# Packed values times first-layer weights: one 64x32 matmul per head instead of one masked 128x64 matmul per pair of heads

## The chip, the core and the metric

The kernel runs on one core of a Trainium2 chip, in float32. The metric is the time of one execution in device microseconds. The engines are named as in the profile: PE (TensorE matmul) and PEld (its weight loads), DVE (VectorE), ACT (ScalarE), POOL (GpSimd) and SP (SyncE, which issues the DMAs).

## The reference

```python
def sm_attn(qq, kk, vv):                      # softmax attention, per batch and head
    s = scale * np.matmul(qq, kk.transpose(0, 1, 3, 2))
    a = np.exp(s - np.max(s, axis=-1, keepdims=True))
    a = a / (np.sum(a, axis=-1, keepdims=True) + 1e-09)
    return np.matmul(a, vv)
p_packed = sm_attn(p, k, v)                   # (8, 8, 32, 64): 8 batches, 8 heads, 32 packed rows
out = sm_attn(q, p_packed, p_packed)          # (8, 8, 576, 64)
x = out.transpose(0, 2, 1, 3).reshape(4608, 512)
h = x @ moe_w_in;   x = (h * np.cos(h)) @ moe_w_out              # 512 -> 2048 -> 512
h = x @ moe2_w_in;  y = (h * np.tanh(softplus(h))) @ moe2_w_out  # the same sizes
```

## The kernel before

**Stage one** covers the attention and the first feed-forward layer, **stage two** the second layer. The second attention has only 32 keys per head, so the kernel never forms `out`. It multiplies the packed values of every head with the head's 64 rows of `moe_w_in` first, which gives for each batch a matrix of 8 x 32 = 256 rows and 2048 columns, called W1 here. The hidden layer is then W1 transposed times the attention weights `aT` (256 x 288 for a half batch).

Stage one walks 256 steps: 16 half batches `t` of 288 tokens, 16 blocks `s` of 128 hidden columns each. A step issues the first product (`l1`, six 128x288 matmuls), the elementwise chain to h*cos(h), and the second product (`l2`, twelve matmuls) three steps later. All of them split float32 into a high and a low part and use three matmuls in `mm3` (lines 140 to 142). Background work is hung onto steps by tables of numbers (`at_pe`, `at_ew`, `at_ld`): the packed attention (`k_unit`, 16 units of one batch and four heads), the attention weights (`q_unit`), the conversion of weights, and the W1 products (`w_unit`). The order on each engine is not the order of the code: a scheduler that plays the program through a timeline places every instruction, with the priorities that `tc.high_priority` gives.

**The W1 products.** `k_unit` ends in stage `s6`: `xt` (128 x 128 in PSUM) holds the packed values of four heads transposed, its 64 value rows twice, one copy in partitions 0 to 63 and one in 64 to 127. Line 299 copies half of it to `PS` on ACT, for the scores of `q_unit` (line 354). Line 305 multiplies two 128x64 slices with `mask` on DVE into `PW`, in which a 128x64 block holds two heads block-diagonally. `w_unit` takes 128 rows of `moe_w_in` (two heads) and 512 columns, and multiplies a 128x64 block of `PW` with them (line 492). Two such matmuls, in the two 64-column halves of the array, fill one PSUM tile of the ring of four (`ring`, shared with `l1`, the scores and the transpositions): W1 of four heads (group `g`) and 512 columns (`fg`). Line 503 copies the tile to `wab` on ACT, line 504 takes the low part on DVE. In the table of groups by line one such matmul has two records.

For batch 0 the matmuls stand in the first steps, with freshly converted weights; for batch 1 around steps 28 to 40; batches 2 and 3, 4 and 5, 6 and 7 are made in pairs, with weights loaded back from DRAM (`ws`, `ld`), 8 sets a pair: a set is one `fg` and `g` for both batches, four matmuls, two PSUM tiles. In one set the two matmuls of a tile, and the first matmuls of the two tiles, use different halves of the array.

**Stage two** has 9 blocks of 512 tokens, 16 steps each: twelve 128x512 matmuls with moving operand `xr`/`xt` (blocks 0, 2, 4, 6, 8) or `xh` (blocks 1, 3, 5, 7), and twelve that accumulate with `wo` moving and `gh` stationary. `xh`, `gg` and `gh` lie in the pool `bpool`, opened when stage one's pool is closed, at the same place. In the built program `bpool` begins at byte 164352 of a partition (642 x 256) and `gap_b` takes its first 192 bytes, so that `gg`, `gh` and `xh` begin 192 bytes behind a multiple of 256; `xr`, `xt`, `wo` and `wab` begin at multiples of 256.

Of the kernel before, what the change touches and what calls it, by code (L numbers as in the profile page):

```python
# [8 lines left out]
F32 = mybir.dt.float32  # L9
F32R = mybir.dt.float32r  # L10
# [21 lines left out]
W_LD = 2  # L32
# [24 lines left out]
W_D = 0  # L57
# [18 lines left out]
PERM = ((0, 1, 2, 3), (2, 3, 0, 1))  # L76


def build(tc, q, k, v, p, w1i, w1o, w2i, w2o, out):
    nc = tc.nc  # L80
    ctx = ExitStack()
    with ctx:
# [29 lines left out]
        mask = wpool.tile([128, 64], F32, name="mask")  # L112
        nc.vector.memset(mask, 0.0)
        for a in range(2):
            nc.vector.memset(mask[64 * a : 64 * a + 64, 32 * a : 32 * a + 32], 1.0)
# [40 lines left out]
        PS = {}  # L156
        PW = {}
        lastexp = [None]

        def k_unit(b, g, alloc_v):  # L160
# [135 lines left out]
            def s6_ew():  # L296
                if b not in PS:
                    PS[b] = ap.tile([128, 128], F32, tag="psp", bufs=3, name=nm("psp"))
                nc.scalar.copy(PS[b][64 * g : 64 * g + 64], st["xt"][64 * g : 64 * g + 64, :128])
                if (b // 2, g) not in PW:  # L300
                    PW[(b // 2, g)] = ap.tile([128, 2, 2, D], F32, tag=f"pw{g}", bufs=2 - g, name=nm("pw"))
                pw = PW[(b // 2, g)]
                for sp in range(2):
                    i = sp if par == 0 else 1 - sp
                    nc.vector.tensor_tensor(pw[:, i, sp], st["xt"][:, 64 * sp : 64 * sp + 64], mask, ALU.mult)
# [14 lines left out]
        def q_unit(t, pre=None):  # L320
# [28 lines left out]
            def s2_pe():  # L349
                st["s"] = [ring() for _ in range(2)]  # L350
                for l in range(4):
                    h = PERM[b % 2][l]
                    for g in range(2):
                        nc.tensor.matmul(  # L354
                            st["s"][g][32 * l : 32 * l + 32, :TT],
                            PS[b][64 * g : 64 * g + 64, 32 * l : 32 * l + 32],
                            st["kt"][64 * g : 64 * g + 64, TT * h : TT * h + TT],
                            start=True,
                            stop=True,
                        )  # L360
# [103 lines left out]
        whalf = {}  # L464

        def w_unit(pair, fg, hp, bp, fresh=False, m=None):
            st = {} if m is None else m
            g, i = hp // 2, hp % 2
            cs = []

            if fresh:
                load, cs = conv(
                    w1i[128 * hp : 128 * hp + 128, 512 * fg : 512 * fg + 512],
                    [128, 512],
                    None,
                    lambda d: w1s.__setitem__((fg, hp), d),
                    "wo" if fg == 0 else True,
                    st,
                )
                cs = cs[:-1]  # L480
            else:

                def load():
                    st["m"] = ld_tile([128, 512])
                    nc.sync.dma_start(st["m"], w1s[(fg, hp)])

            def pe():
                if i == 0:
                    whalf[(bp, fg, g)] = ring()
                ps = whalf[(bp, fg, g)]  # L490
                pos = bp ^ i
                nc.tensor.matmul(  # L492
                    ps[64 * pos : 64 * pos + 64], PW[(pair, g)][:, i, pos], st["m"], start=True, stop=True
                )

            def ew():
                if i == 0:
                    return
                ps = whalf.pop((bp, fg, g))
                w = W1.get((2 * pair + bp, fg))  # L500
                if w is None:
                    w = W1[(2 * pair + bp, fg)] = wab_tile(bp, [128, 2, 2, 512], F32R)
                nc.scalar.copy(w[:, g, 0], ps)
                nc.vector.tensor_tensor(w[:, g, 1], ps, w[:, g, 0], ALU.subtract)

            return load, cs, pe, ew
# [99 lines left out]
        place(stages, [PRO + Q0_T + i for i in range(2)] + [PRO + Q0 + i for i in range(6)], HP_PRO)  # L606
        for j in range(16):
            load, cs, pe, ew = w_unit(0, j // 4, j % 4, 0, True)
            n = W0_STEP[j]
            at_ld(n - W0_LD if j >= 4 else PRO + W0E[j], load)  # L610
            for i, f in enumerate(cs):
                at_ew(n - 3 + i, f)
            at_pe(n, pe)
            at_ew(n, ew)
# [12 lines left out]
        for j in range(16):  # L627
            load, cs, pe, ew = w_unit(0, j // 4, j % 4, 1)
            n = W01[0] + int(W01[1] * j)
            at_ld(n - W_LD, load)  # L630
            at_pe(n, pe)
            at_ew(n, ew)
# [18 lines left out]
        for pair in range(3):  # L651
# [9 lines left out]
            for j in range(16):  # L661
                m = {}
                n = n0 + W_POS[pair][0] + int(W_POS[pair][1] * (j // 2 * 2 + 1))
                at_ld(n - W_LD - 1 + j % 2, w_unit(pair + 1, j // 4, j % 4, 0, m=m)[0])
                for bp in range(2):
                    _, _, pe, ew = w_unit(pair + 1, j // 4, j % 4, bp, m=m)
                    at_pe(n + W_D * bp, pe)
                    at_ew(n + W_D * bp, ew)
# [155 lines left out]
        bp.tile([128, 48], F32, name="gap_b")  # L824
# [90 lines left out]
```

## Time and profile before

| | us |
|---|---|
| median of 3 runs (1653.84 to 1654.74) | 1654.02 |
| the profiled execution | 1651.3 |
| its span, first to last instruction | 1649.5 |
| PE busy in it | 1588.2 |
| DVE, ACT, POOL busy | 717.9, 762.2, 365.0 |

The profiled execution is the one whose rows are read here; 1.8 us lie around its span. Stage one ends near 850 us of the span. PE is busy nearly without a break after the first 150 us; DVE and ACT are half busy in stage one and little in stage two. The DMA engines are nearly full for the first 150 us.

### The profile page before, as it was taken

What the parts mean: (1) busy time and instruction counts of PE and PEld (TensorE: products, weight loads), DVE (VectorE), ACT (ScalarE), POOL (GpSimd) and SP (SyncE); (2) the same over time, 40 slices, a digit from 0 to 9 for tenths busy, and PEclk for the clock granted to TensorE, in tenths of its full rate; (3) what the DMA queues carried; (4) which work ended last, traced back from release to release, by engine and by line L of the source; (5) the groups of instructions that cost most, each with busy time, mean ns of one, the idle gap of its engine ahead of it and who ended that gap; (6) DMA issues with size and microseconds to landing.
All of it is one profiled execution on the core that took longest, in us unless ns stands there. A gap on an engine that the chain in (4) does not pass through costs nothing.

```text
span 1649.5 us, 25389 instructions
## 1 busy us (share of the span) xinstructions
PE 1588.2 (96%) x9568; PEld 1324.5 (80%) x9568; DVE 717.9 (44%) x1529; ACT 762.2 (46%) x1510; POOL 365.0 (22%) x376
## 2 busy tenths in 40 slices
PE   3879999999999999999999999999999999999999
PEld 1667777799878997889898888888888888888887
DVE  5986665666657666687761111111111111111111
ACT  3676576666656666667772222322222222222221
POOL 0552223343323333244660010101010101000000
PEclk9899999999999999999999999999999999999999
DMA  9979565533544343353340010101010101010000
GB/s 285 305 192 237 152 189 135 136 79 86 162 113 99 89 124 127 98 187 117 111 131 0 16 36 1 52 0 51 1 52 1 51 0 52 1 52 1 8 18 26
DMA packets 101115, 147.42 MB, mean 89 GB/s; under 512 B 25728, under 2 KB 51328, under 8 KB 100992
## 3 DMA queue, kind: packets, MB, share of 16 engines
q1 hardware_dynamic: 100992, 145.79, 31.1%
q8 instruction: 75, 1.23, 0.3%
q14 instruction: 48, 0.39, 0.1%
HBM read 114.29 MB, written 31.46 MB: 88 GB/s over the span
## 4 chain that ended last, share of the span: by engine, by line
PE 84%; DMA 7%; DVE 4%; ACT 2%; issue 2%; SPq 1%; POOL 0%; DVEq 0%; ACTq 0%; POOLq 0%
PE acc L140 15%; PE acc L141 14%; PE acc L142 14%; PE ps L140 12%; PE ps L141 11%; PE ps L142 11%; PE ps L492 3%; DMA kr<-in_k_dram 1%; DMA kr<-in_q_dram 1%; DMA raw<-in_moe_w_out_dram 1%; PE ps L354 1%; DMA ld<-ws 1%; PE ps L214 1%; PE ps L275 1%; DVE r L719 1%
## 5 line engine op out<-in xcount | busy, mean ns | idle before, releaser
L856 DVE TENSOR_TENSOR gh<-gg,gh 128x512 fp32r<-128x512 f32 x144 | 105.7, 734 | 623.6 <-ACT gh L855 623.5
L849 ACT ACTIVATE gg<-ps 128x512 f32<-128x512 f32 x144 | 86.1, 598 | 550.4 <-PE ps L142 550.4
L729 POOL TENSOR_TENSOR gh<-r,gh 128x288 fp32r<-128x288 f32 x256 | 215.6, 848 | 396.4 <-ACT gh L726 288.6
L141 PE MATMUL acc<-gh,wo 128*128 128x288 f32 x1024 | 301.9, 300 | 0.3
L142 PE MATMUL acc<-gh,wo 128*128 128x288 f32 x1024 | 297.8, 298 | 0.0
L140 PE MATMUL acc<-gh,wo 128*128 128x288 f32 x1024 | 284.3, 305 | 1.7 <-ACT gh L726 1.7
L141 PE MATMUL acc<-wo,gh 128*128 128x512 f32 x576 | 227.2, 394 | 0.0
L140 PE MATMUL acc<-wo,gh 128*128 128x512 f32 x576 | 226.7, 394 | 0.0
L142 PE MATMUL acc<-wo,gh 128*128 128x512 f32 x576 | 225.0, 391 | 0.0
L140 PEld LDWEIGHTS acc<-gh,wo 128*128 128x128 f32 x1024 | 184.7, 190 | 38.7 <-issue 18.0
L141 PEld LDWEIGHTS acc<-gh,wo 128*128 128x128 f32 x1024 | 194.6, 190 | 8.8 <-issue 4.6
L142 PEld LDWEIGHTS acc<-gh,wo 128*128 128x128 f32 x1024 | 193.4, 190 | 6.3 <-issue 4.6
L140 PE MATMUL ps<-aT,wab 128*128 128x288 f32 x512 | 160.5, 314 | 17.0 <-DVE r L719 10.9
L718 ACT ACTIVATE r<-r,halfpi 128x288 f32<-128x288 f32 x256 | 135.7, 535 | 78.4 <-DVE r L712 75.9
L709 ACT ACTIVATE ki<-ps,quarter 128x288 int32<-128x288 f32 x256 | 125.5, 496 | 83.4 <-PE ps L142 73.4
L141 PE MATMUL ps<-aT,wab 128*128 128x288 f32 x512 | 152.9, 299 | 0.0
L142 PE MATMUL ps<-aT,wab 128*128 128x288 f32 x512 | 152.5, 298 | 0.0
L719 DVE TENSOR_TENSOR r<-r,ps 128x288 f32<-128x288 f32 x256 | 113.9, 449 | 69.1 <-ACT r L718 68.7
L711 DVE SCALAR_TENSOR_TENSOR r<-ki,ps 128x288 f32<-128x288 int32 x256 | 113.9, 448 | 55.8 <-ACT ki L709 46.5
L140 PEld LDWEIGHTS ps<-aT,wab 128*128 128x128 f32 x512 | 97.9, 192 | 39.1 <-DVE r L719 20.2
L140 PEld LDWEIGHTS acc<-wo,gh 128*128 128x128 f32 x576 | 108.2, 188 | 25.1
L142 PEld LDWEIGHTS acc<-wo,gh 128*128 128x128 f32 x576 | 108.2, 188 | 24.8
(124 smaller groups left out, 2579.2 us busy)
## 6 DMA issues: line engine op xcount, KB each, us to landing
ld<-ws SPq DMA_DIRECT2D x96, 256.0 KB, 2.9
kr<-in_k_dram SPq DMA_DIRECT2D x64, 272.0 KB, 5.7
raw<-in_moe_w_out_dram SPq DMA_DIRECT2D x32, 512.0 KB, 4.8
kr<-in_q_dram SPq DMA_DIRECT2D x60, 272.0 KB, 5.5
x2d<-xo SPq DMA_DIRECT2D x64, 144.0 KB, 1.8
out_dram<-ld SPq DMA_DIRECT2D x36, 256.0 KB, 2.0
raw<-in_moe_w_in_dram SPq DMA_DIRECT2D x16, 512.0 KB, 5.7
ws<-tmp SPq DMA_DIRECT2D x32, 256.0 KB, 4.8
```

The costliest lines, as they stand in the source:

```text
L140: nc.tensor.matmul(ps, l0, r0, start=first, stop=False)
L141: nc.tensor.matmul(ps, l0, r1, start=False, stop=False)
L142: nc.tensor.matmul(ps, l1, r0, start=False, stop=last)
L214: nc.tensor.matmul(st["s1"][x][32 * l : 32 * l + 32, :TT].rearrange("p (s a) -> p a s", a=9), st["pp"][64 * x : 64 * x + 64, 32 * h : 32 * ...
L492: nc.tensor.matmul(ps[64 * pos : 64 * pos + 64], PW[(pair, g)][:, i, pos], st["m"], start=True, stop=True)
L709: nc.scalar.activation(ki, st["h"], AF.Identity, bias=quarter, scale=1.0 / TWO_PI)
L711: nc.vector.scalar_tensor_tensor(r, ki, -TWO_PI, st["h"], ALU.mult, ALU.add)
L718: nc.scalar.activation(g, g, AF.Sin, bias=halfpi, scale=1.0)
L719: nc.vector.tensor_tensor(g, g, st["h"], ALU.mult)
L729: nc.gpsimd.tensor_tensor(gh[:, 1], st["g"], gh[:, 0], ALU.subtract)
L849: nc.scalar.activation(g, st["h"], AF.Mish)
L856: nc.vector.tensor_tensor(gh[:, 1], st["g"], gh[:, 0], ALU.subtract)
```

## The change

The masks and `PW` go. `s6` makes one copy of all of `xt` to `PK` on ACT (128 partitions instead of 64), and both the scores and the W1 products read it. `w_unit` now takes one matmul per head: 64 rows of `PK` (a head's values), 32 columns, 512 columns of weights moving. Its rows of the array are the head's parity (`r`), its columns the place `l`; `PERM` is changed so that the two batches of a pair have opposite rows at each `l`. A set of a pair is thus eight matmuls in eight places of the array, a set of batch 0 or 1 four. Each of the two PSUM tiles of a set is written from both halves of the array's rows, at different partitions. For batches 0 and 1 both halves of a tile are issued at one step, the later one. `w_load` takes the loads out of `w_unit`; the steps of loads and of matmuls of pairs stay. `gap_b` goes; with the 256 bytes of `mask` gone too, `bpool` begins at byte 164096 (641 x 256) and `gg`, `gh` and `xh` at multiples of 256.

```diff
-W_D = 0
-PERM = ((0, 1, 2, 3), (2, 3, 0, 1))
+PERM = ((0, 2, 1, 3), (1, 3, 0, 2))
...
-        mask = wpool.tile([128, 64], F32, name="mask")
-        nc.vector.memset(mask, 0.0)
-        for a in range(2):
-            nc.vector.memset(mask[64 * a : 64 * a + 64, 32 * a : 32 * a + 32], 1.0)
...
-        PS = {}
-        PW = {}
+        PK = {}
...
             def s6_ew():
-                if b not in PS:
-                    PS[b] = ap.tile([128, 128], F32, tag="psp", bufs=3, name=nm("psp"))
-                nc.scalar.copy(PS[b][64 * g : 64 * g + 64], st["xt"][64 * g : 64 * g + 64, :128])
-                if (b // 2, g) not in PW:
-                    PW[(b // 2, g)] = ap.tile([128, 2, 2, D], F32, tag=f"pw{g}", bufs=2 - g, name=nm("pw"))
-                pw = PW[(b // 2, g)]
-                for sp in range(2):
-                    i = sp if par == 0 else 1 - sp
-                    nc.vector.tensor_tensor(pw[:, i, sp], st["xt"][:, 64 * sp : 64 * sp + 64], mask, ALU.mult)
+                PK[(b, g)] = ap.tile([128, 128], F32, tag=f"pk{g}", bufs=4, name=nm("pk"))
+                nc.scalar.copy(PK[(b, g)], st["xt"][:, :128])
...
-                            PS[b][64 * g : 64 * g + 64, 32 * l : 32 * l + 32],
+                            PK[(b, g)][64 * g : 64 * g + 64, 32 * l : 32 * l + 32],
...
-        def w_unit(pair, fg, hp, bp, fresh=False, m=None):
...
+        def w_unit(bs, fg, g, ms):
+            st = {}
 
             def pe():
-                if i == 0:
-                    whalf[(bp, fg, g)] = ring()
-                ps = whalf[(bp, fg, g)]
-                pos = bp ^ i
-                nc.tensor.matmul(
-                    ps[64 * pos : 64 * pos + 64], PW[(pair, g)][:, i, pos], st["m"], start=True, stop=True
-                )
+                for b in bs:
+                    st[b] = ring()
+                for x in range(4):
+                    for b in bs:
+                        for l, h in enumerate(PERM[b % 2]):
+                            if l == x:
+                                r = 64 * (h % 2)
+                                nc.tensor.matmul(
+                                    st[b][32 * l : 32 * l + 32],
+                                    PK[(b, g)][r : r + 64, 32 * l : 32 * l + 32],
+                                    ms[h // 2]["m"][r : r + 64],
+                                    start=True,
+                                    stop=True,
+                                )
 
             def ew():
-                if i == 0:
-                    return
-                ps = whalf.pop((bp, fg, g))
-                w = W1.get((2 * pair + bp, fg))
-                if w is None:
-                    w = W1[(2 * pair + bp, fg)] = wab_tile(bp, [128, 2, 2, 512], F32R)
-                nc.scalar.copy(w[:, g, 0], ps)
-                nc.vector.tensor_tensor(w[:, g, 1], ps, w[:, g, 0], ALU.subtract)
+                for b in bs:
+                    w = W1.get((b, fg))
+                    if w is None:
+                        w = W1[(b, fg)] = wab_tile(b % 2, [128, 2, 2, 512], F32R)
+                    nc.scalar.copy(w[:, g, 0], st[b])
+                    nc.vector.tensor_tensor(w[:, g, 1], st[b], w[:, g, 0], ALU.subtract)
...
-                for bp in range(2):
-                    _, _, pe, ew = w_unit(pair + 1, j // 4, j % 4, bp, m=m)
-                    at_pe(n + W_D * bp, pe)
-                    at_ew(n + W_D * bp, ew)
+                if j % 2:
+                    pe, ew = w_unit((b0, b0 + 1), j // 4, j % 4 // 2, (ms[j - 1], ms[j]))
+                    at_pe(n, pe)
+                    at_ew(n, ew)
...
-        bp.tile([128, 48], F32, name="gap_b")
```

The scheduler then orders everything anew. On PE, the second set of batches 2 and 3 (`ps` tiles and `pw` or `pk` tiles of the two batches, `ld` the weights) stood like this before:

```order
L141 MATMUL acc3_576_2832<-gh_645_3182,wo_201_907 128x288
L492 MATMUL ps_660_3244<-ld_638_3146,pw_476_2299 64x512
L492 MATMUL ps_660_3244<-ld_652_3202,pw_476_2299 64x512
L492 MATMUL ps_661_3246<-ld_638_3146,pw_476_2299 64x512
L492 MATMUL ps_661_3246<-ld_652_3202,pw_476_2299 64x512
L142 MATMUL acc3_576_2832<-gh_645_3182,wo_201_907 128x288
```

and now:

```order
L137 MATMUL ps_658_3250<-aT_507_2475,wab_462_2258 128x288
L482 MATMUL ps_659_3257<-ld_638_3158,pk_474_2311 32x512
L482 MATMUL ps_659_3257<-ld_651_3215,pk_474_2311 32x512
L482 MATMUL ps_660_3258<-ld_638_3158,pk_548_2709 32x512
L482 MATMUL ps_660_3258<-ld_651_3215,pk_548_2709 32x512
L482 MATMUL ps_659_3257<-ld_638_3158,pk_474_2311 32x512
L482 MATMUL ps_660_3258<-ld_638_3158,pk_548_2709 32x512
L482 MATMUL ps_659_3257<-ld_651_3215,pk_474_2311 32x512
L482 MATMUL ps_660_3258<-ld_651_3215,pk_548_2709 32x512
L136 MATMUL acc0_573_2841<-gh_645_3198,wo_200_914 128x288
```

Four rows have become eight, still in one piece. A set of batches 4 and 5 on PE before:

```order
L142 MATMUL acc3_1050_5406<-gh_1075_5562,wo_164_746 128x288
L492 MATMUL ps_1096_5666<-ld_1077_5568,pw_785_3899 64x512
L492 MATMUL ps_1097_5668<-ld_1077_5568,pw_785_3899 64x512
L492 MATMUL ps_1096_5666<-ld_1086_5612,pw_785_3899 64x512
L492 MATMUL ps_1097_5668<-ld_1086_5612,pw_785_3899 64x512
L140 MATMUL acc0_1047_5403<-gh_1083_5602,wo_178_799 128x288
L140 MATMUL ps_1103_5702<-aT_1005_5177,wab_707_3509 128x288
```

and now:

```order
L136 MATMUL acc2_1049_5441<-gh_1083_5642,wo_175_798 128x288
L482 MATMUL ps_1096_5706<-ld_1077_5604,pk_784_3939 32x512
L482 MATMUL ps_1096_5706<-ld_1086_5652,pk_784_3939 32x512
L482 MATMUL ps_1096_5706<-ld_1077_5604,pk_784_3939 32x512
L482 MATMUL ps_1096_5706<-ld_1086_5652,pk_784_3939 32x512
L137 MATMUL acc2_1049_5441<-gh_1083_5642,wo_175_798 128x288
L135 MATMUL acc3_1050_5442<-gh_1083_5642,wo_175_798 128x288
L482 MATMUL ps_1097_5707<-ld_1077_5604,pk_985_5127 32x512
L482 MATMUL ps_1097_5707<-ld_1086_5652,pk_985_5127 32x512
L135 MATMUL ps_1103_5746<-aT_1005_5213,wab_706_3538 128x288
```

Here the set is in pieces: four matmuls of one tile, two of the other after two rows of the second product, and the last two twelve rows further on. By the built programs the sets of the three pairs stand in 36 pieces on PE before (14 of four matmuls, 22 of one or two) and in 38 now (16 of five to eight, 22 of one to four); those of batch 1 in 9 and 9, those of batch 0 in 9 and 10.

On DVE, the stretch ahead of the first hidden block, from the last fresh weights of the first tile (`wab_69`, now `wab_68`) to the half of `wo` that completes the second tile, before:

```order
L444 SCALAR_TENSOR_TENSOR wab_69_362<-wab_69_362 128x512
L504 TENSOR_TENSOR wab_65_344<-ps_57_324,wab_65_344 128x512
L383 TENSOR_REDUCE sqs_58_326<-tmp_48_296 128x18
L384 TENSOR_SCALAR sqs_58_326<-sqs_58_326 128x18
L504 TENSOR_TENSOR wab_80_397<-ps_73_373,wab_80_397 128x512
L386 RECIPROCAL rq_59_329<-sqs_58_326 128x18
L440 TENSOR_SCALAR wo_55_319<-wo_53_312 128x512
L444 SCALAR_TENSOR_TENSOR wo_55_319<-wo_55_319 128x512
L391 STREAM_TRANSPOSE tmp_64_342<-tmp_48_296 128x576
```

and now:

```order
L431 SCALAR_TENSOR_TENSOR wab_68_357<-wab_68_357 128x512
L496 TENSOR_TENSOR wab_63_335<-ps_61_328,wab_63_335 128x512
L370 TENSOR_REDUCE sqs_56_315<-tmp_47_287 128x18
L371 TENSOR_SCALAR sqs_56_315<-sqs_56_315 128x18
L373 RECIPROCAL rq_57_318<-sqs_56_315 128x18
L427 TENSOR_SCALAR wo_54_310<-wo_52_303 128x512
L378 STREAM_TRANSPOSE tmp_62_333<-tmp_47_287 128x576
L431 SCALAR_TENSOR_TENSOR wo_54_310<-wo_54_310 128x512
```

The subtraction into `wab_80` has left the stretch, the transposition of line 391 stands in front of the last `wo` row, and the four multiplications of line 305, which stood 8 and 15 rows ahead, are gone.

## Rows read from the trace of the kernel before

**Rows 1.** The page's busy line and its first line of 40 slices.
```profile
PE 1588.2 (96%) x9568; PEld 1324.5 (80%) x9568; DVE 717.9 (44%) x1529; ACT 762.2 (46%) x1510; POOL 365.0 (22%) x376
...
PE   3879999999999999999999999999999999999999
```

**Rows 2.** Stretches: bounds, length, busy us of each engine, granted clock, DMA share, GB/s.
```profile
0.00:60.00 60.00, 28.68 (x208) 16.41 (x209) 39.31 (x89) 28.07 (x57) 13.35 (x16) 0.91 0.97 292
60.00:120.00 60.00, 50.31 (x336) 39.03 (x335) 55.09 (x105) 40.99 (x84) 32.92 (x29) 0.94 0.83 232
265.00:330.00 65.00, 64.83 (x455) 47.51 (x452) 39.76 (x95) 39.31 (x82) 19.94 (x22) 1.00 0.48 124
625.00:700.00 75.00, 75.00 (x512) 59.47 (x511) 47.34 (x108) 47.35 (x98) 23.89 (x29) 1.00 0.31 94
900.00:1650.00 750.00, 745.94 (x3242) 608.53 (x3241) 109.19 (x152) 190.10 (x314) 35.86 (x28) 1.00 0.07 23
```

**Rows 3.** What TensorE waited for: total us, times, longest.
```profile
PE ps L492 <- DVE wo L444: 4.3, 1, 4.3
```

**Rows 4.** The same stretches for line 492 alone: TensorE, weight load, clock, DMA.
```profile
265.00:330.00 65.00, 17.00 (x64) 3.60 (x60) 1.00 0.48 124
...
625.00:700.00 75.00, 16.16 (x64) 3.61 (x64) 1.00 0.31 94
```

**Rows 5.** TensorE's order of time around a set of four (start us, length, line, tile).
```profile
629.25 0.30 PE L142 MATMUL acc<-gh,wo 128*128 128x288 f32 x1
629.48 1.94 PE L492 MATMUL ps<-ld,pw 128*64 128x512 f32 x8
631.35 0.40 PE L140 MATMUL acc<-gh,wo 128*128 128x288 f32 x1
631.59 0.30 PE L141 MATMUL acc<-gh,wo 128*128 128x288 f32 x1
```

**Rows 6.** The same around a pair of one set.
```profile
640.89 0.29 PE L142 MATMUL acc<-gh,wo 128*128 128x288 f32 x1
641.12 1.08 PE L492 MATMUL ps<-ld,pw 128*64 128x512 f32 x4
642.12 0.40 PE L140 MATMUL acc<-gh,wo 128*128 128x288 f32 x1
642.36 0.29 PE L141 MATMUL acc<-gh,wo 128*128 128x288 f32 x1
```

**Rows 7.** The same around the eight 64x32 score matmuls of line 354.
```profile
687.79 0.30 PE L142 MATMUL acc<-gh,wo 128*128 128x288 f32 x1
688.02 0.72 PE L354 MATMUL ps<-kt,psp 64*32 64x288 f32 x16
688.67 0.40 PE L140 MATMUL acc<-gh,wo 128*128 128x288 f32 x1
688.91 0.29 PE L141 MATMUL acc<-gh,wo 128*128 128x288 f32 x1
```

**Rows 8.** Stage two, TensorE's order of time, moving operand xh.
```profile
941.53 0.39 PE L140 MATMUL ps<-xh,wab 128*128 128x512 f32 x1
...
943.16 0.39 PE L141 MATMUL ps<-xh,wab 128*128 128x512 f32 x1
```

**Rows 9.** The same, moving operands xr and xt.
```profile
1030.63 0.39 PE L140 MATMUL ps<-xr,wab 128*128 128x512 f32 x1
...
1032.90 0.39 PE L141 MATMUL ps<-xt,wab 128*128 128x512 f32 x1
```

**Rows 10.** The same, the second product (moving wo, stationary gh).
```profile
1199.44 0.39 PE L141 MATMUL acc<-wo,gh 128*128 128x512 f32 x1
...
1201.73 0.39 PE L142 MATMUL acc<-wo,gh 128*128 128x512 f32 x1
```

**Rows 11.** A group by line: busy us, mean ns, idle before and its releaser.
```profile
L305 DVE TENSOR_TENSOR pw<-ps,mask 128x64 f32<-128x64 f32 x32 | 5.6, 217 | 6.3 <-ACT psp L299 6.3
```

More of the change, by code (lines that the diff above doesn't have):

```diff
@@ L463, in build, with w_load @@
         w1s = {}
-        whalf = {}
-        def w_unit(pair, fg, hp, bp, fresh=False, m=None):
-            st = {} if m is None else m
-            g, i = hp // 2, hp % 2
-            cs = []
+        def w_load(fg, hp, fresh=False):
+            st = {}
             if fresh:
@@ L479, in w_unit, with load @@
                 )
[L480 to L485, printed above, removed]
-            def pe():
-                if i == 0:
-                    whalf[(bp, fg, g)] = ring()
-                ps = whalf[(bp, fg, g)]
-                pos = bp ^ i
-                nc.tensor.matmul(
-                    ps[64 * pos : 64 * pos + 64], PW[(pair, g)][:, i, pos], st["m"], start=True, stop=True
-                )
-            def ew():
-                if i == 0:
-                    return
-                ps = whalf.pop((bp, fg, g))
-                w = W1.get((2 * pair + bp, fg))
-                if w is None:
-                    w = W1[(2 * pair + bp, fg)] = wab_tile(bp, [128, 2, 2, 512], F32R)
-                nc.scalar.copy(w[:, g, 0], ps)
-                nc.vector.tensor_tensor(w[:, g, 1], ps, w[:, g, 0], ALU.subtract)
-            return load, cs, pe, ew
+                return st, load, cs[:-1]
+            def load():
+                st["m"] = ld_tile([128, 512])
+                nc.sync.dma_start(st["m"], w1s[(fg, hp)])
+            return st, load, []
+        def w_unit(bs, fg, g, ms):
+            st = {}
+            def pe():
+                for b in bs:
[12 more added lines that the diff above has]
+                                )
+            def ew():
+                for b in bs:
[4 more added lines that the diff above has]
+                    nc.vector.tensor_tensor(w[:, g, 1], st[b], w[:, g, 0], ALU.subtract)
+            return pe, ew
         WO = {}
@@ L606, in build @@
         place(stages, [PRO + Q0_T + i for i in range(2)] + [PRO + Q0 + i for i in range(6)], HP_PRO)
+        ms = {}
         for j in range(16):
-            load, cs, pe, ew = w_unit(0, j // 4, j % 4, 0, True)
+            ms[j], load, cs = w_load(j // 4, j % 4, True)
             n = W0_STEP[j]
@@ L612, in build @@
                 at_ew(n - 3 + i, f)
-            at_pe(n, pe)
-            at_ew(n, ew)
+            if j % 2:
+                pe, ew = w_unit((0,), j // 4, j % 4 // 2, (ms[j - 1], ms[j]))
+                at_pe(n, pe)
+                at_ew(n, ew)
         for ft in range(16):
@@ L627, in build @@
         for j in range(16):
-            load, cs, pe, ew = w_unit(0, j // 4, j % 4, 1)
+            ms[j], load, _ = w_load(j // 4, j % 4)
             n = W01[0] + int(W01[1] * j)
             at_ld(n - W_LD, load)
-            at_pe(n, pe)
-            at_ew(n, ew)
+            if j % 2:
+                pe, ew = w_unit((1,), j // 4, j % 4 // 2, (ms[j - 1], ms[j]))
+                at_pe(n, pe)
+                at_ew(n, ew)
         pre = []
@@ L661, in build @@
             for j in range(16):
-                m = {}
+                ms[j], load, _ = w_load(j // 4, j % 4)
                 n = n0 + W_POS[pair][0] + int(W_POS[pair][1] * (j // 2 * 2 + 1))
-                at_ld(n - W_LD - 1 + j % 2, w_unit(pair + 1, j // 4, j % 4, 0, m=m)[0])
-                for bp in range(2):
-                    _, _, pe, ew = w_unit(pair + 1, j // 4, j % 4, bp, m=m)
-                    at_pe(n + W_D * bp, pe)
-                    at_ew(n + W_D * bp, ew)
+                at_ld(n - W_LD - 1 + j % 2, load)
+                if j % 2:
+                    pe, ew = w_unit((b0, b0 + 1), j // 4, j % 4 // 2, (ms[j - 1], ms[j]))
+                    at_pe(n, pe)
+                    at_ew(n, ew)
         for t in range(1, NT):
```

## The prediction, made before the changed kernel was run

> **What bounds the kernel now.** I read the page's busy line and slices first. The reader is to see one engine near its limit: PE at 96% of the span, DVE and ACT below half, and PE's slices at 9 from the third on [rows 1]. Next the stretches, because a share over the whole span mixes them. In the first 60 us PE works 28.7 and waits 31.3, in the next 60 it waits 9.7 while DVE works 55.1: there PE is not the bound, loads and DVE are. From 265 us on PE has no idle time worth naming (64.8 of 65, 75.0 of 75), while DVE and ACT work some 60% of it, and stage two looks the same with 745.9 of 750 [rows 2]. Last, line 492 by stretch: 17.0 us busy at 265 to 330 and 16.2 at 625 to 700 [rows 4]; the pair between them lies alike. What PE is spared in these three stretches should come off the time one for one; what it is spared in the first 120 us should not.
>
> **The change part by part.**
>
> *The W1 products of the three pairs.* What one piece of them costs PE is the delay that it puts between its neighbours. The neighbours follow each other at 0.13 us (in the 128x288 stream the starts before and behind show it). From the last start before a set of four to the second start behind it are 631.59 - 629.25 = 2.34 us; two undisturbed steps would be 0.26, so the set costs 2.08 [rows 5]. A pair of matmuls costs 642.36 - 640.89 - 0.26 = 1.21 [rows 6]. The difference, 0.87, is one more round: the four use two places of the array twice, and what uses the same place waits. Pieces of one matmul cost the same 1.21, since a round has one length.
>
> For eight matmuls in eight places the trace has a near relative, the scores of line 354: 64x32 in eight places, moving 288 instead of 512. They cost 688.91 - 687.79 - 0.26 = 0.86 [rows 7]. One matmul has two records, and one record of 288 columns at this pace is shorter than one of 512 in proportion: 1.21 minus 0.86 is 0.35, and 224 more columns, twice, at the pace of line 492 (0.87 for 512 columns) are 0.38. So the eight behave as a single round, with at most some 0.05 on top. I take 1.26 for a piece of five to eight and 1.21 for a smaller one.
>
> Now the pieces as the built orders have them. Before: 14 x 2.08 + 22 x 1.21 = 55.7 us. As a check, the busy time in the two stretches shown averages 16.6, which makes 49.8 for three pairs, and 36 pieces with some 0.14 of gap at their edges add 5.0: 54.8. After: 16 x 1.26 + 22 x 1.21 = 46.8. The term is **-9.0 us**. It would be 55.7 - 24 x 1.26 = 25.5 if each of the 24 sets stood in one piece. They do not, as the second of the order's places shows, and every cut costs a full round.
>
> *Batches 0 and 1.* A set goes from two matmuls to four, in one round either way. Batch 1 stands in 9 pieces on PE before and after: nothing. Batch 0 goes from 9 to 10 pieces, in a stretch where PE waits 31 us anyway: nothing.
>
> *The start.* Before, the last half of the second tile waits 4.3 us for the converted weights, `wo` of line 444 [rows 3], and the first hidden block follows it. DVE works without a break ahead of it. Four multiplications of 0.217, 0.87 us, leave that stretch [rows 11]. A subtraction leaves it too and a transposition that waits for POOL comes in, which I set against each other. So the first hidden block comes 0.9 us earlier at best. Behind it loads set the pace (DMA share 0.97 and 0.83 [rows 2]), and the order of SP's loads of fresh weights and of `w_out` between the first batches has changed. The bounds: -3.5 if the 16 multiplications of batches 0 to 3, 16 x 0.217, were all on the path; and +5, half of the 9.7 that PE waits at 60 to 120 once more. I take 0, near the 0.9, since the loads behind it come no sooner.
>
> *ACT's copy* grows from 64 to 128 partitions at the same 128 columns. Partitions work side by side, and ACT has slack: nothing. The copies also no longer go ahead of a DVE multiplication, which only shortens the way to the first W1 product.
>
> *The filler tile.* PE runs stage two without idle time [rows 2], so its pace is its time. With `xh` moving, seven steps take 943.16 - 941.53 = 1.63 us, 0.233 each [rows 8]. With `xr` and `xt`, ten steps take 2.27, 0.227 each [rows 9]. Shapes, weights and what runs beside them are the same; what differs in the program is the address, 192 bytes behind a multiple of 256 against a multiple of 256. The change puts `xh` on a multiple of 256. Four blocks x 16 steps x 12 = 768 matmuls x 0.0059 = **-4.5 us**. The second product, 10 steps in 2.29 [rows 10], 0.229 each, has its stationary `gh` at the odd place and moving `wo` at an even one; if it too went to 0.227, 1728 x 0.002 = 3.5 more would go. On the other side, if it is the distance between two tiles and not the place of one that counts, the penalty of `xh` could move to the second product: 1728 x 0.004 = 7 us more. I take the value that has two operands of this trace behind it, -4.5, and keep -8 and +7.
>
> **The sum.** Against the profiled execution: 1651.3 - 9.0 - 4.5 = 1637.8. The median of the runs shown lies 2.7 above that execution, so against the median 1654.0 - 13.5 = **1640.5 us**.
>
> **The rivals.**
>
> *The address makes no difference* (the slow `xh` comes from its pool's place among the others, which stays). For it speaks that no second tile at such an odd place shows a moving operand; against it, that nothing else differs between the rows. Time: 1654.0 - 9.0 = 1645.
>
> *The beginning gains as well.* In the order before, three ring tiles of batch 0 are held half filled while several hidden blocks pass; now a tile is filled at one step, and `l1` finds rings sooner. PE's 9.7 us of waiting at 60 to 120 could shrink by 5, and the second product by 3.5: 1632. Against it speaks that DVE works 55 of those 60 us.
>
> *The new order costs what the rounds give.* The place is the first 265 us, where PE waits for DVE, ACT and loads; the price is the 41 us it waits in the first 120 [rows 2], a fourth more of which is 10. It decides once a late weight load holds the first blocks of batch 0. 1640.5 + 10 = 1650. An address penalty that only moves gives about the same: 1654.0 - 9.0 + 7 = 1652.
>
> *Two halves of the array's rows do not write one PSUM tile together: slower.* In no matmul of the trace before do they: the scores write each half into a tile of its own [rows 7], line 492 used all rows. If matmuls of the two halves took turns at a tile, of the 38 pieces of the pairs 25 would take two rounds and 5 three (by their order and places), 35 rounds more at 0.87 = 30.5 us; 8 of batch 1's 9 pieces would take one more, 7.0. The first 9.0 gained turn into 28.5 lost, and with the filler's part the time is 1654.0 + 28.5 - 4.5 = 1678. It decides from 11 extra rounds on. Against it speaks that the two halves write different partitions of the tile.
>
> A page bears on this one. The Trainium skill says in "TensorEngine Tiling (Array Packing)", Restrictions and Gotchas, that different row tiles cannot access the same PSUM bank at the same time; by this rule the change would be slower. "PSUM — Partial Sum Buffer", section PSUM bank collisions, adds that the hardware does not arbitrate or stall in a collision, and counts a collision by bank and 32-partition quadrant; by that sentence there is no turn-taking, and the time stays at 1640. No run here shows either yet.
>
> **How the numbers follow.** The forecast, with a few microseconds either way at the start, 1634 to 1648: 45%. No effect of the address, 1645: 20%. More gained at the beginning, 1632: 10%. The new order or a moved penalty eats the gain, 1650 to 1656: 16%. Turns at the PSUM tile, 1678: 7%. Something else that makes it slower: 2%. The range 1632 to 1654 leaves out the last two, half of the tenth case and a part of the fourth. A measurement of this kernel can tell about 0.2%, 3.3 us, from no change: faster is below 1650.7. That is 45 + 20 + 10 and a fourth of the fourth, 79%; slower, above 1657.3, 9% and 1 of the fourth; the rest, 11%, between.
>
> **What would show it.** In the changed profile, the busy time of the new W1 line in the three pairs' stretches should be near 38 x 1.1 = 42 us, a set of eight in one piece about 1.1 us long, and a piece of four of one tile no longer than that. If such a piece takes 1.9, the turns are there. The step of `xh` in stage two should be 0.227; 0.233 refutes the filler's term. PE's idle time before 265 us should be within 5 us of what it is now; if it has grown by 10 or more, the new order is the cause, and the waits of PE there name the engine. If stage one ends less than 5 us earlier although the pieces are as short as forecast, the rounds were not on the path.

## The result and the profile after

The changed kernel takes 1637.44 us (median of 4 runs, 1635.1 to 1641.63), the kernel before beside it 1654.38 (1653.84 to 1655.77): a ratio of 0.9899, 95% interval 0.9878 to 0.992. The forecast was 1640.5, the range 1632 to 1654. The profiled execution took 1637.47 us with a span of 1635.7, 13.8 less than the one of before. Line numbers have moved: `mm3` is now lines 135 to 137, the W1 matmul line 482.

The page's busy line and first slices, beside [rows 1]:

```profile
PE 1568.1 (96%) x9824; PEld 1318.6 (81%) x9824; DVE 715.7 (44%) x1494; ACT 760.5 (46%) x1510; POOL 363.2 (22%) x376
...
PE   3879999999999999999999999999999999999999
```

PE's busy time fell by 20.1, DVE's by only 2. The stretches of after, columns as in [rows 2]:

```profile
0.00:60.00 60.00, 27.50 (x203) 12.54 (x204) 34.10 (x75) 25.32 (x51) 9.70 (x14) 0.89 0.90 267
60.00:120.00 60.00, 47.99 (x335) 36.75 (x334) 54.45 (x97) 39.84 (x82) 31.65 (x28) 0.88 0.79 235
265.00:330.00 65.00, 64.10 (x560) 50.79 (x558) 44.12 (x101) 43.89 (x92) 22.31 (x25) 1.00 0.52 134
625.00:700.00 75.00, 74.08 (x574) 58.02 (x573) 47.84 (x108) 48.59 (x98) 25.82 (x29) 1.00 0.28 91
```

PE now has 0.9 us of idle time in each of the pairs' stretches, where it had 0.2 and none [rows 2]. The W1 line alone there (TensorE, weight load, clock, DMA), beside [rows 4]:

```profile
265.00:330.00 65.00, 11.82 (x128) 1.83 (x128) 1.00 0.52 134
448.00:535.00 87.00, 14.80 (x128) 2.20 (x124) 1.00 0.40 104
625.00:700.00 75.00, 14.93 (x128) 2.21 (x128) 1.00 0.28 91
```

That is 41.5 us; "near 42" was forecast. Of the two shown before, 17.0 became 11.8 and 16.2 became 14.9; with the third, 17.5, they made 50.6 before. TensorE's order of time around a piece of four matmuls of one tile, written from both halves of the rows, and around a set of eight:

```profile
455.56 0.29 PE L136 MATMUL acc<-gh,wo 128*128 128x288 f32 x1
455.78 1.06 PE L482 MATMUL ps<-ld,pk 64*32 64x512 f32 x8
456.78 0.40 PE L137 MATMUL acc<-gh,wo 128*128 128x288 f32 x1
457.01 0.29 PE L135 MATMUL acc<-gh,wo 128*128 128x288 f32 x1
...
465.33 0.29 PE L135 MATMUL acc<-gh,wo 128*128 128x288 f32 x1
465.56 1.09 PE L482 MATMUL ps<-ld,pk 64*32 64x512 f32 x16
466.57 0.40 PE L136 MATMUL acc<-gh,wo 128*128 128x288 f32 x1
466.81 0.29 PE L137 MATMUL acc<-gh,wo 128*128 128x288 f32 x1
```

Worked out as for [rows 5] and [rows 6], the eight cost 466.81 - 465.33 - 0.26 = 1.22 and the four 457.01 - 455.56 - 0.26 = 1.19. Both are one round; the halves do not take turns at a tile. Of the twelve sets that stand in one piece ten take 1.09. One takes 1.38, and one, at 627.75, two rounds (2.32), with a wait of 0.19 for DVE `r` between its halves.

To split the time between the stages I take the start of the first `xr` matmul as the border (line, count, ns shortest/median/longest, first and last start). Before:

```profile
L140 PE MATMUL ps<-xr,wab x10: 389/389/395, 851.1 to 865.4; 128*128 128x512 f32 x10
```

After:

```profile
L135 PE MATMUL ps<-xr,wab x12: 389/389/395, 848.6 to 868.3; 128*128 128x512 f32 x12
```

Stage one thus took 851.1 and 848.6 us, stage two 1649.5 - 851.1 = 798.4 and 1635.7 - 848.6 = 787.1. Of the 13.8 us, 11.3 come from stage two and 2.5 from stage one, the reverse of the forecast 4.5 and 9.0. The 2.5 is one pair of executions; more of them are compared further down, under the size of the rounds' term. The matmuls with `xh` moving, from 870 to 1610, before:

```profile
870.00:1610.00 740.00, 190.23 (x768) 144.03 (x768) 7.46 (x12) 15.48 (x12) 1.00 0.07 22
```

and after:

```profile
870.00:1610.00 740.00, 185.12 (x768) 144.16 (x768) 7.46 (x12) 15.31 (x12) 1.00 0.07 22
```

The 768 matmuls take 5.1 us less. The second product has become faster too; after, ten of its steps take 1199.02 - 1196.76 = 2.26, against 2.29 in [rows 10]:

```profile
1196.76 0.39 PE L135 MATMUL acc<-wo,gh 128*128 128x512 f32 x1
...
1199.02 0.39 PE L136 MATMUL acc<-wo,gh 128*128 128x512 f32 x1
```

Stage one as a whole (columns as in [rows 2]: length, then PE's busy time first), before:

```profile
0.00:851.10 851.10, 793.36 (x6112) 675.57 (x6113) 599.09 (x1365) 555.94 (x1170) 322.31 (x343) 0.98 0.54 151
```

and after:

```profile
0.00:848.60 848.60, 784.63 (x6369) 670.16 (x6370) 599.05 (x1330) 554.38 (x1170) 320.82 (x343) 0.98 0.54 152
```

PE works 8.7 us less there and idles 64.0 instead of 57.7.

### The profile page after: what moved, and what is told of

The parts are those of the page before. It is cut to its first block, busy times and chain, and to the rows that moved or that the text cites. A ratio compares the mean times of both kernels' runs of the same rounds, so it can differ in the third digit from the quotient of the medians.

```text
span 1635.7 us, 25860 instructions
## 1 busy us (share of the span) xinstructions
PE 1568.1 (96%) x9824; PEld 1318.6 (81%) x9824; DVE 715.7 (44%) x1494; ACT 760.5 (46%) x1510; POOL 363.2 (22%) x376
## 4 chain that ended last, share of the span: by engine, by line
PE 81%; DMA 7%; DVE 6%; ACT 3%; issue 2%; POOL 0%; SPq 0%; DVEq 0%; ACTq 0%; POOLq 0%
PE acc L135 14%; PE acc L136 14%; PE acc L137 14%; PE ps L135 11%; PE ps L136 11%; PE ps L137 11%; PE ps L482 3%; DMA kr<-in_k_dram 2%; DMA raw<-in_moe_w_out_dram 1%; DVE r L709 1%; DVE r L708 1%; DMA raw<-in_moe_w_in_dram 1%; DMA kr<-in_q_dram 1%; ACT r L715 1%; PE ps L341 1%
## 5 line engine op out<-in xcount | busy, mean ns | idle before, releaser
L135 PE MATMUL ps<-aT,wab 128*128 128x288 f32 x512 | 160.5, 314 | 15.7 <-DVE r L716 10.3
L723 ACT CAST gh<-r 128x288 fp32r<-128x288 f32 x256 | 108.3, 428 | 46.8 <-DVE r L716 25.0
L136 PEld LDWEIGHTS acc<-wo,gh 128*128 128x128 f32 x576 | 108.2, 188 | 22.5
```

Of the source, the lines that this page charges most:

```text
L135: nc.tensor.matmul(ps, l0, r0, start=first, stop=False)
L136: nc.tensor.matmul(ps, l0, r1, start=False, stop=False)
L723: nc.scalar.copy(gh[:, 0], st["g"])
```

## The experiments

Each ran beside the kernel before. The executions of one kernel scatter by some microseconds, above all through the start, so the lengths of the stages in the profiled executions are compared as well: stage two repeats to 0.1 us in the traces of like kernels.

**1. The filler tile alone, both ways (e1, e2).** From the kernel before the tile `gap_b` is taken out; to the changed kernel one of the same size is added. The order of every engine stays.

```diff
-        bp.tile([128, 48], F32, name="gap_b")     # e1, from the kernel before
+        bp.tile([128, 48], F32, name="gap_b")     # e2, to the changed kernel
```

> The kernel before with only the filler tile gap_b taken out, so that xh, gg and gh of stage two begin at multiples of 256 bytes; the order of all instructions stays. Theory (the place of a tile against a multiple of 256 bytes sets TensorE's pace): about 11 us less than before, 1643.5, all of it in stage two, xh steps 0.227 and second product 0.227 instead of 0.233 and 0.229. Rival (stage two became faster because something of the new first-layer code let it, or because the tiles lie nearer to others): the time of before, 1654, within 2 us.

> The changed kernel with the filler tile of 192 bytes put back, nothing else; the order of all instructions stays. Theory (place against 256 bytes): about 11 us more than the changed kernel, 1648, with xh steps at 0.233 again. Rival: 1637, as the changed kernel.

Before without the filler: 1644.94 us, ratio 0.9935 (0.9914 to 0.9955). After with it: 1651.12, ratio 0.9982 (0.9964 to 0.9999). The medians thus moved by 9.1 and 13.7. By the traces stage two took 787.1 and 798.4, exactly what the place of the tiles says, whatever stage one is. The `xh` matmuls without the filler in the old kernel (190.23 with it):

```profile
870.00:1610.00 740.00, 185.11 (x768) 144.20 (x768) 7.45 (x12) 15.23 (x12) 1.00 0.07 22
```

So the filler's part is 11.3 us of stage two, and it is the place that does it. Without the filler the pool begins at byte 164352 in the old kernel and at 164096 in the new one, an even and an odd multiple of 256; both give 787.1. The first of them also measured what luck there is at the start: with the same order as before, its stage one took 856.0 instead of 851.1.

**2. Which tile's place (e5, e10).** In the changed kernel `xh` alone, then `gh` alone, is put 192 bytes behind a multiple of 256 (the lines are shortened; in e10 the 64 bytes ahead of `xh` make the 192 up to 256, so that `xh` stays at a multiple).

```diff
+   bpool[0].tile([128, 48], F32, name="gap_x")   # e5, ahead of the first xh
+   bp.tile([128, 48], F32, name="gap_g")         # e10, ahead of the first gh (16 floats ahead of xh)
```

> The changed kernel (1637.4, stage two 787.3 us by its trace) with 192 bytes put ahead of xh alone, so that xh begins 192 bytes behind a multiple of 256 while gg and gh stay at multiples; the order of every engine is the changed kernel's. Theory (each operand read by TensorE is slower off a multiple of 256, the moving xh and the stationary gh each by its own place): the xh steps go back to 0.233 and the second product stays at 0.227, stage two 791.8, median about 1642 (1639 to 1645). Rival 1 (the gain belongs to the second product, xh followed from what runs between): stage two stays at 787.3, median 1637. Rival 2 (any operand of the pool off the multiple slows both products): stage two 798.6, median 1649.

> The changed kernel with the stationary tiles gh of stage two alone 192 bytes behind a multiple of 256; gg and xh stay at multiples. In the kernel before, where gh and xh both lie there, the second product's steps are 0.2292 in the blocks of xr and 0.2321 in those of xh; with xh alone off, they are 0.2267 and 0.2286. Theory (a misplaced tile costs its own matmuls and some of those right behind them, and the costs of the two tiles add): second product 0.2292 in the blocks of xr and about 0.230 in those of xh, xh steps 0.2267; stage two 787.1 + 1728 x 0.0025 = 791.5 to 793, median 1641 to 1645. Rival (the stationary tile's place counts for nothing, the slow second product of before came from gg, which ACT and DVE read beside it): stage two 787.1, median 1637.

1645.84 us (ratio 0.9938, 0.9918 to 0.9957) and 1644.04 (0.9937, 0.9914 to 0.996); stage two 793.6 and 791.0. With `xh` off, its 768 matmuls are back at the old time:

```profile
870.00:1610.00 740.00, 190.18 (x768) 143.87 (x768) 7.45 (x12) 15.47 (x12) 1.00 0.07 22
```

With `gh` off they stay:

```profile
870.00:1610.00 740.00, 185.08 (x768) 144.19 (x768) 7.46 (x12) 15.25 (x12) 1.00 0.07 22
```

and the second product's ten steps are at 2.29 again (1202.53 - 1200.24):

```profile
1200.24 0.39 PE L135 MATMUL acc<-wo,gh 128*128 128x512 f32 x1
...
1202.53 0.40 PE L136 MATMUL acc<-wo,gh 128*128 128x512 f32 x1
```

Means of all recorded steps of stage two from 860 to 1620 us, worked out from the starts in the order of time, in us; a step runs from a matmul's start to the next start (second product: in blocks of `xr` / of `xh`):

| kernel | bytes off a multiple of 256 | `xh` step | second product | `xr` step | stage two |
|---|---|---|---|---|---|
| before | `gg`, `gh`, `xh` 192 | 0.2333 | 0.2290 / 0.2318 | 0.2268 | 798.4 |
| after | none | 0.2267 | 0.2267 / 0.2267 | 0.2267 | 787.1 |
| e5 | `xh` 192 | 0.2333 | 0.2267 / 0.2284 | 0.2266 | 793.6 |
| e10 | `gh` 192 | 0.2266 | 0.2290 / 0.2290 | 0.2267 | 791.0 |
| e6 | all three 128 | 0.2321 | 0.2330 / 0.2321 | 0.2308 | 804.3 |
| e9 | all three 64 | 0.2318 | 0.2332 / 0.2332 | 0.2314 | 804.5 |

The theory held for the cost of `gh` on its own matmuls, and `gg` off its place adds nothing to them (0.2290 in the blocks of `xr` before too, where `gg` was off). For `xh` it fell short: its own matmuls cost 768 x 0.0066 = 5.1, and the second product, with both operands in place, costs 768 x 0.0017 = 1.3 more in its blocks. In the mean over these blocks of that run the six steps behind an `xh` group take 227, 235, 229, 233, 231 and 226 ns, the six after them 226 to 228: the delay is carried into the matmuls that follow. With `gh` off by 192 nothing is carried: the first product's steps stay at 0.2266 and 0.2267, and that part of e10's theory fell.

**3. Other distances (e6, e9).** The changed kernel with 128 and with 64 bytes ahead of `gg`, `gh` and `xh`.

```diff
+        bp.tile([128, 32], F32, name="gap_b")     # e6; [128, 16] in e9
```

> The changed kernel with 128 bytes put ahead of the pool of gg, gh and xh, so that all three begin 128 bytes behind a multiple of 256; the order is the changed kernel's. Theory (only a multiple of 256 is fast; a row of 2048 bytes that begins off it costs the same whatever the offset): stage two 798.6, median about 1649. Rival 1 (a multiple of 128, or of 64, is enough and 192 is slow for another reason): for 128 stage two stays at 787.3, median 1637. Rival 2 (the cost grows with the distance from the nearest multiple, 64 bytes in the kernel before, 128 here): stage two longer than 798.6, up to 810, median up to 1660.

> The changed kernel (stage two 787.1 us from the first xr matmul to the end) with 64 bytes put ahead of gg, gh and xh; the order is the changed kernel's. So far: 192 bytes off 798.4, 128 bytes off 804.3. Theory A (it is the distance to the nearest multiple of 256 that counts, 64 and 192 are alike): stage two 798, xh steps 0.233, median about 1649 to 1652. Theory B (it is the place within 256 bytes, each with its own cost): neither 787 nor 798; by no row can its size be said, up to 804.

1657.95 us (ratio 1.0008, 0.9993 to 1.0022) and 1656.69 (1.0008, 0.9995 to 1.0021); stage two 804.3 and 804.5. 64 and 192 are equally far from a multiple of 256 and 6.1 us apart, so distance does not explain it, and neither does one cost for every place off a multiple: each place has its own (theory B of e9), and only the multiple of 256 is free among the four tried. Here even `xr` is slower, though its tile is not moved (five steps take 1.16, 0.232 each; e6):

```profile
1032.68 0.40 PE L135 MATMUL ps<-xr,wab 128*128 128x512 f32 x1
...
1033.84 0.40 PE L137 MATMUL ps<-xr,wab 128*128 128x512 f32 x1
```

That would fit a delay carried over from `gh`, though at 192 bytes `gh` carries none; what carries it no view shows.

**4. The old start (e3).** Batches 0 and 1 as before, with masked matmuls of two heads issued at two steps each; the pairs and the place of the tiles as in the changed kernel.

```diff
-            if j % 2:
-                pe, ew = w_unit((0,), j // 4, j % 4 // 2, (ms[j - 1], ms[j]))
-                at_pe(n, pe)
-                at_ew(n, ew)
+            pe, ew = w_old(j // 4, j % 4, 0, ms[j])
+            at_pe(n, pe)
+            at_ew(n, ew)
```

> The changed kernel with the old masked matmuls (and mask, and copies) for batches 0 and 1 only; the three pairs keep the eight matmuls per set, and no filler tile. TensorE's order of the first 155 us is that of before. Theory (the new order at the start costs 8 us by the first output copy, of which some 5 are got back by 180 us, and the rest stays): 3 to 8 us less than the changed kernel, 1629 to 1634; first output copy near 122 us instead of 130. Rival (the late start comes from how long the loads of that one execution took, not from the order): 1637, and the first output copy near 130 here as well.

1641.37 us, ratio 0.9919 (0.9893 to 0.9945); stage one 852.1. The theory fell: the old start is not faster than the new. PE's idle time up to 265 us is 50.9, against 50.7 in the changed kernel, and 47.7 and 50.3 in two runs of the old order (before, and before without filler). The new order of the start costs nothing that can be told from the scatter.

**5. Whole sets (e4).** A one-column write to the two tiles and an order in which seven matmuls come behind the first (not shown) tie the eight together, and priority 160 puts each set in one piece: 24 pieces instead of 38.

```diff
+                if len(bs) > 1:
+                    for b in bs:
+                        nc.vector.memset(st[b][:, :1], 0.0)
...
-                    at_pe(n, pe)
+                    at_pe(n, hp(pe, 160))
```

> The changed kernel with every set of the three pairs held together: a one-column VectorE write to both PSUM tiles of a set ahead of its matmuls, seven of the eight matmuls ordered behind the first, and a higher priority for the set. 24 pieces on TensorE instead of 38. Theory (each piece costs a full round of 1.2 us on TensorE, which is the bound there): 14 x 1.2 = 17 us less than the changed kernel, 1620. Rival 1 (pieces were not on the path in the second and third pair, where other waits came in): 0 to 6 us less, 1631 to 1637. Rival 2 (two ring tiles held until both are free starve the first product): slower than the changed kernel.

1634.03 us, ratio 0.9873 (0.9852 to 0.9893): 3.4 below the changed kernel instead of some 17. The W1 line did what was asked (8.72 in each stretch, 24 x 1.09 in all):

```profile
265.00:330.00 65.00, 8.72 (x128) 1.47 (x128) 1.00 0.54 143
448.00:535.00 87.00, 8.72 (x128) 1.52 (x128) 1.00 0.40 104
625.00:700.00 75.00, 8.72 (x128) 1.45 (x128) 1.00 0.34 105
```

but PE has 3.9, 4.3 and 5.7 us of idle time in the same stretches:

```profile
265.00:330.00 65.00, 61.14 (x593) 50.33 (x590) 44.15 (x117) 45.10 (x94) 23.22 (x26) 1.00 0.54 143
448.00:535.00 87.00, 82.66 (x751) 69.70 (x750) 55.84 (x151) 57.85 (x124) 29.19 (x33) 1.00 0.40 104
625.00:700.00 75.00, 69.33 (x583) 58.42 (x582) 52.69 (x129) 49.24 (x99) 24.99 (x28) 1.00 0.34 105
```

What PE mostly waits for from 265 to 830 us is the ring tile of a hidden block that DVE's last multiplication, cosine by `h` (`r`, line 728 here), frees:

```profile
PE ps L135 <- DVE r L728: 17.1, 12, 2.8
```

For the same wait the changed kernel has

```profile
PE ps L135 <- DVE r L716: 9.3, 11, 2.1
```

and the kernel before

```profile
PE ps L140 <- DVE r L719: 8.1, 12, 2.2
```

One such place, 3.2 us behind the end of a set: one first product (six matmuls) has been issued since, the next finds no tile free.

```profile
641.95 1.09 PE L488 MATMUL ps<-ld,pk 64*32 64x512 f32 x16
...
646.26 0.40 PE L135 MATMUL ps<-aT,wab 128*128 128x288 f32 x1 [1.17 <-DVE r L728]
```

The set's own two tiles are copied later still; on ACT two table loads of 1.28 and the hidden blocks' work come first:

```profile
641.57 1.28 ACT L366 ACT_TABLE_LOAD   x1
...
643.89 1.28 ACT L727 ACT_TABLE_LOAD   x1
...
646.58 1.07 ACT L507 CAST wab<-ps 128x512 fp32r<-128x512 f32 x2
```

**6. Are the rounds on the path (e7)?** To the whole sets of experiment 5: each set is issued twice in its piece (one of the 24 came out in three pieces).

```diff
-                for x in range(4):
+                for x in tuple(range(4)) * len(bs):
```

> The whole sets of the experiment before (24 pieces of eight, 1634.0, stage one 844.2 by its trace), with each set of the three pairs issued twice in the same piece, so that 24 pieces of 16 take two rounds each: 24 x 0.87 = 20.9 us more TensorE work in the pairs' stretches, nothing else. Theory (the rounds that the changes took from TensorE only partly came off the time, because the chain of ring tiles, DVE and ACT behind the first product then sets the pace of these stretches): TensorE's idle time of 13.9 us in the stretches 265 to 330, 448 to 535 and 625 to 700 takes up most of the extra rounds, median 1634 + 7 to 1634 + 13, and the idle time there falls below 5 us. Rival (a round is on the path one for one, and the whole sets gave little for another reason, such as a late start): 1634 + 20.9 = 1655, the idle time stays near 14 us.

1657.83 us, ratio 1.0012 (1.0000 to 1.0025). By the traces stage one grew from 844.4 to 863.6, 19.2 of the 20.9 added; PE's idle time in stage one is 74.2 against 73.9. The medians lie further apart, 23.8, since the profiled execution was the shortest of its ten. A piece of sixteen has length 1.95:

```profile
273.66 1.95 PE L488 MATMUL ps<-ld,pk 64*32 64x512 f32 x32
275.54 0.40 PE L135 MATMUL ps<-aT,wab 128*128 128x288 f32 x1
```

The theory fell and the rival held: a round costs its full time, if not a little more, and the idle time of whole sets is neither filled by longer sets nor made by short ones. The loss of whole sets is a price of its own, about 11 us (idle 20.3 against 9.3 between 150 and 700).

**7. Who frees the ring tiles late?** The copies of the pairs' W1 tiles get the matmuls' priority (e8), and then DVE makes half of them (e11).

```diff
-                    at_ew(n, ew)
+                    at_ew(n, hp(ew, 160))
...
+                    if len(bs) > 1 and b % 2:
+                        nc.vector.tensor_copy(w[:, g, 0], st[b])
+                    else:
+                        nc.scalar.copy(w[:, g, 0], st[b])
```

> The whole sets (1634.0) with ACT's copies and DVE's subtractions of the pairs' W1 tiles given the same high priority as their matmuls, so that the ring tiles come free sooner. Theory A (TensorE waits for the first product's ring tiles because W1 tiles hold two of the four for 3.6 us after the set): the 13.9 us of idle time in the three stretches shrink by half or more, median 1624 to 1629. Theory B (the elementwise chain is late by the work that the early copies put ahead of it, and the wait moves to the hidden blocks' own range reduction): the idle time stays within 3 us of 13.9, median 1632 to 1638.

> The whole sets with early copies, where DVE instead of ACT makes the first copy of the second batch's tile of each pair set, so that a ring tile comes free without waiting for ACT and its table loads. Theory (TensorE's idle time with whole sets, 20 us at 150 to 700 against 9 of the changed kernel, is the first product's wait for ring tiles that ACT frees late): the idle time falls to 10 to 15 and the median to 1625 to 1630. Rival (the wait is for the range reduction of the hidden blocks, DVE r, which the copies on DVE only put later): idle 18 to 25, median 1632 to 1640.

1634.88 us (ratio 0.987, 0.9842 to 0.9899) and 1631.9 (0.9864, 0.9838 to 0.9889). PE's idle time from 150 to 700 is 20.1 and 20.9, as with plain whole sets (20.3): theory A and the theory of e11 fell; what stood against them held, though e11's median lies 0.1 below the range given there. The second is the fastest kernel of the study, with stage one at 842.1, but its interval overlaps that of the plain whole sets.

## Why the prediction was right, and where its sizes were not

**The rounds.** The step held as stated: one round of 1.2 us for any piece, no turns. The piece of four of one tile, written by both halves of the rows, took 1.06 us, no longer than a pair of before (1.08 [rows 6]). The Trainium skill's "TensorEngine Tiling (Array Packing)", Restrictions and Gotchas, says that different row tiles cannot access the same PSUM bank at once; the trace does not agree. The Trainium skill's "PSUM — Partial Sum Buffer", section PSUM bank collisions, counts a collision by bank and 32-partition quadrant; the trace agrees, since the halves write different quadrants and need one round.

**The size of the rounds' term.** -9.0 us of PE work were forecast. Over all profiles of the two orders of stage one, PE's busy time is 793.4 and 795.7 before (two runs), 784.5 to 787.1 after (six runs, mean 785.6): -9.0. But stage one's length went only from a mean of 853.6 to 849.6, -3.9, since PE's idle time rose from 59.0 to 64.1. The timed executions say the same: their spans less stage two of the trace make stage one 855.3 in the mean of 49 of the old order (before, e1) and 851.0 in that of 42 of the new one (after, e2, e5, e6, e9, e10), 4.3 less, with 1.1 either way at 95% if they are taken as independent.

Two other reasons for PE's smaller work can be set aside. The granted clock over the first 120 us, a mean over stretches at 2.4 and at 1.2 GHz, is 0.93 in before and in e2 and 0.89 in after; between before and e2 PE's work falls by 8.9, its idle time rises by 5.2 and stage one gets 3.7 shorter, so the clock is not the reason. Nor is it the place of tiles: in the built programs the tiles of both products of stage one (`aT`, `wab`, `gh`, `wo`) begin at multiples of 256 before and after.

What failed is "what PE is spared in these three stretches should come off the time one for one". A round is worth its full time by experiment 6; but the new order of the pieces comes with new waits. After 265 us PE idles 10.1 and 10.0 in the two runs of the old order, and 11.8 to 14.9 (mean 13.5) in the six of the new one; this part repeats. Of these 3.4 us more, 2.0 are the wait for DVE `r` (8.1 and 7.1 in the old order, 9.0 to 10.3 in the new one); the others are short waits on other engines. That the order makes them, and not the shorter work alone, is argued from experiment 6 and not shown for this kernel. The whole sets show the same trade larger: against the changed kernel 14.1 us less PE work in stage one (770.5), 9.9 more idle time, 4.2 gained. The other 1.6 us of idle time lie before 265 us, where two runs of one order differ by 2.7; they can't be laid on the change.

**The start** was taken as 0 with bounds -3.5 and +5; experiment 4 finds no difference. **Batches 0 and 1** were taken at nothing: batch 1's nine pieces take 1.04 to 1.06 us each, where eight of the nine took 1.07 to 1.08; batch 0 no run measured by itself. **ACT's copy** at nothing was right: over 128 partitions it takes 0.262 us (median of 16), over 64 it took 0.261. DVE and ACT are as busy in stage one as they were (599.1 and 554.4 us, before 599.1 and 555.9).

**The filler's term** had the right mechanism and was too small: -4.5 forecast, -11.3 measured (experiment 1). `xh` itself gives 5.1 instead of 4.5, because its mean step is 0.2333 where seven steps gave 0.2329. The prediction named the second product, 3.5 more, as a bound and left it out of the sum for want of a second operand; it gives 1728 x 0.0023 = 4.0 by `gh` itself (experiment 2), 1.3 that `xh` carries into it, and some 0.8 where both are off (768 x 0.0011, what 0.2318 has above 0.2267 + 0.0023 + 0.0017). These make 11.2 of the 11.3. The fear that the penalty moves to another tile was unfounded.

The two errors, 5 too much in stage one and 6.8 too little in stage two, nearly cancel, and that is luck: 13.5 were forecast against the profiled execution and 13.8 came, and the median is 3.1 below the forecast. The sum was better than its parts. By the criterion that the prediction set, stage one ending less than 5 us earlier with short pieces, the rounds would not be on the path; experiment 6 shows that this reading would have been wrong.

**What stays open.** Why whole sets make PE wait longer for `r`: neither earlier copies nor DVE's copies changed it. A set holds two of the four ring tiles; a longer ring wasn't tried, nor the priority and the one-column write by themselves. And why a delay at a misplaced tile is carried into matmuls whose operands lie well.

## What to carry to other kernels

Count the rounds of small matmuls and the pieces in which the schedule issues them, but do not count on the spared time in full before the waits of the new order are known: compare PE's busy and idle time, not its busy time alone. Here 9.0 us less work gave some 4. Where a long stretch is pure TensorE work, look at where in a partition every moving and stationary tile begins; here 192 bytes cost 11.3 us in 800. Split a result by stage before believing that the forecast's parts were right.

## What the runs showed of the hardware

Matmuls of 128x128 by 512 columns step in stage two at 0.2267 us when all operands begin at multiples of 256 bytes; with tiles 64, 128 or 192 bytes off, means of 0.229 to 0.2333 were seen, at 192 bytes for the moving tile alone (0.2333) and for the stationary tile alone (0.2290). Behind a moving tile 192 bytes off the following matmuls are slowed as well (0.2284, e5); behind a stationary one 192 bytes off they are not (0.2266, e10). Two 64-row halves of the array write different partitions of one PSUM tile at the same time, eight 64x32 matmuls of 512 columns in 1.09 us. And traces of one and the same order of stage one differ by 5 us in its length (851.1 and 856.0): PE's work by 2.3, its waits before 265 us by 2.6.
